# Attention and gated feed-forward on one core: another order of the opening, the last weight in halves, pooling sums of the second batch on GpSimd

## The chip, the cores and the metric

The kernel runs on one core of one Trainium2 chip. The metric is device microseconds from start to end of one launch. The core's engines are TensorE (PE; its weight loads are shown apart as PEld), VectorE (DVE), ScalarE (ACT), GpSimd (POOL) and SyncE (SP), which issues nearly all DMAs. Each engine works through its own list of instructions in order.

## The reference

Eight batches of eight heads, 576 tokens each, head width 64. Keys and values are pooled: the mean of every eight tokens, so 72 pooled positions per head. Then softmax attention, and a gated two-layer product over the 4608 tokens (512 features, 2048 hidden).

```python
k_p = k.reshape(B, H, Sp, pool, D).mean(axis=3)
v_p = v.reshape(B, H, Sp, pool, D).mean(axis=3)
scores = scale * np.matmul(q, k_p.transpose(0, 1, 3, 2))
attn = softmax(scores)                      # max subtracted, 1e-9 in the sum
x = np.matmul(attn, v_p)                    # to (4608, 512)
h = x @ w_in
out = (h * np.clip(h + 3.0, 0.0, 6.0) / 6.0) @ w_out
```

The weights arrive as 64-bit words (view of doubles); everything is computed in 32 bits.

## The kernel before

**Blocks and steps.** The 4608 tokens are cut into 12 blocks (512, 256, then ten of 384). For each block, 16 steps f run over 128 hidden columns each. A step has `h()` (L590: twelve products over four chunks of features, each as high times high, low times high and high times low, where high and low are two 32-bit parts that TensorE multiplies fast), then on ACT and DVE `relu`, `gate`, `hi`, `lo` (L603 to L617), and two steps later `out()` (L619: three products for each 128 tokens, into four sums that stay in PSUM for the whole block). While block j runs its steps, the attention for block j+1 is threaded in between as a list of small pieces (`att_steps`, `Paced`).

**Block 0 is different.** Its attention cannot hide beside another block, and the 16 weights have to be prepared during it. A weight f is 1024 columns: 512 of w_in (part 0) and 512 of w_out (part 1). `Prep` turns a raw weight into high and low parts in six operations: `scale`, `low` and `hi` on ACT, `sign`, `join` and `lo` on DVE. Weight 0 is loaded and prepared in two halves, the others whole. During the steps, step u finishes weight u+1 (`hi`, `lo`), joins weight u+2 and starts weight u+3 (L799 to L814). Two scratch buffers u take turns (f even or odd); they lie in the place of weight 15. So weight 15 can be loaded only when weight 14's `lo` has read its scratch buffer: L809.

**The opening** is one list written out by hand (L676 to L766) under `in_order()`, which ties each instruction on TensorE, DVE and ACT to the one before it in the text on the same engine. GpSimd and SP are not tied; for them, and outside such blocks, a scheduler chooses the order. The opening first sums and scores tokens 0 to 255 of batch 0 (part A), then multiplies with the values (`av`), then does tokens 256 to 511 (part B): score product, maximum (`top`), exponentials (`exps`, four ACT instructions that also give the sums; or `shift`, `exp`, `total`, which puts part of it on DVE), `invert`, `divide`, `transposes`, `av`. Between them stand the preparation of weight 0 and the first halves of step f=0 for part A (`a[0]`). Step f=0 for part B is then the first step of the loop. `busy(n)` (L200) gives TensorE n products of the identity with itself, which nobody reads; 13 stand at the start. PSUM banks for the attention are taken in turn from `att_banks`.

**The pooling sums.** `prep_k` (L139) and `prep_v` (L242) sum every eight tokens. For batch 0 the keys are summed on DVE and the values on TensorE (`FirstValues`: products with the identity, for the 64 first pooled positions in `heads`, for the remaining eight in `rest`, the latter masked on DVE in `place_rest`). For batch 1, needed by block 1 and so computed during block 0's steps, four key sums and six value sums are DVE reductions in the written order. For later batches they are DVE reductions that the scheduler places. After each sum of values GpSimd multiplies with a mask and subtracts the high part (L258, L267, L272). Raw keys and values share a ring of four buffers, so values of batch 1 are loaded as key sums free them.

Of the kernel before, what the change touches and what calls it, by code (L numbers as in the profile page):

```python
# [30 lines left out]
def attention_moe_kernel(  # L31
# [104 lines left out]

    ksum = {}

    def prep_k(b, p):  # L139
# [4 lines left out]
        with in_order() if b == 1 else nullcontext():  # L144
            nc.vector.tensor_reduce(
                out=ks[:, i], in_=kraw.pop((b, p)).rearrange("p (s o) -> p s o", o=POOL), axis=AX.X, op=ALU.add
            )
# [57 lines left out]
    class FirstValues:  # L205
# [27 lines left out]
        def place_rest(self):  # L233
            for g in range(NG):
                nc.vector.tensor_tensor(
                    out=self.vrem[:, g].rearrange("p (h d) -> p h d", h=4),
                    in0=self.pr[:, g, None, :].broadcast_to([REM, 4, D]),
# [4 lines left out]
    def prep_v(b, p):  # L242
# [9 lines left out]
        with in_order() if b == 1 else nullcontext():  # L252
            nc.vector.tensor_reduce(  # L253
                out=vs, in_=st[:n, : POOL * D].rearrange("p (o d) -> p d o", o=POOL), axis=AX.X, op=ALU.add
            )
# [150 lines left out]
    def put_x(j, T, x0, p, ps):  # L406
        xhi, xlo = (t[:, p, x0 : x0 + T] for t in x_block(j))
        nc.scalar.copy(xhi, ps)  # L408
        nc.vector.tensor_tensor(out=xlo, in0=ps, in1=xhi.bitcast(F32), op=ALU.subtract)  # L409

    def av(j, b, h0, T, x0, p):
# [4 lines left out]
        put_x(j, T, x0, p, ps)  # L416
# [48 lines left out]
    def groups(f):  # L465
        return [(0, 1), (1, 2)] if f < SPLIT else [(0, 2)]

    def w_tile(name, f, a, b, shape, dtype):
        return const.tile([P, b - a] + shape, dtype, name=f"{name}_{f}", tag=f"w_{f}_{a}" if f < SPLIT else f"w_{f}")

    def load_w(f):
        wraw[f] = []
# [7 lines left out]
    class Prep:  # L480
# [10 lines left out]
        def __init__(self, f):  # L491
            self.f, self.raws, self.made = f, wraw.pop(f), {}
            if f == 0:
                ubuf.append(const.tile([P, 2, 2 * DM], F32, name="u", tag=f"w_{NF - 1}"))
            if f == NF - 1:
                _, _, raw = self.raws[0]
                self.parts = [(i, i + 1, raw[:, i : i + 1], ring("u")[:, :DM]) for i in range(2)]
            else:
                u = ubuf[0][:, f % 2]
                self.parts = [(a, b, raw, u[:, a * DM : b * DM]) for a, b, raw in self.raws]  # L500
# [59 lines left out]

    def prep(f, *stages, part=None):
        if f not in preps:
            preps[f] = Prep(f)
        parts = preps[f].parts
        for s in stages:
            for x in parts if part is None else parts[part : part + 1]:
                getattr(preps[f], s)(x)
# [107 lines left out]
    a = [Step(first, f, 0, 2) for f in range(SPLIT)]  # L675
    with in_order():  # L676
# [4 lines left out]
        for x in (x00, x10, x01, x11):  # L681
            x.product()
        x00.top()
# [20 lines left out]
        values.rest()  # L704
        values.place_heads()
        T0, T1 = tiles(A)
        transposes(*T0, 0, 0)
        transposes(*T1, 0, 0)
        values.place_rest()
        prep(0, "scale", "low", part=0)  # L710
        transposes(*T0, 1, 0, nc.scalar.copy)
        transposes(*T1, 1, 0, nc.scalar.copy)
        prep(0, "sign", "join", "hi", "lo", part=0)
        av(0, *A, 0)
        prep(0, "scale", part=1)
        av(0, *A, 1)
        prep(0, "low", part=1)
        av(0, *A, 2)
        av(0, *A, 3)
        prep(0, "sign", "join", "hi", part=1)  # L720
        att_banks[:] = ["a0", "a1", "o2", "o3"]
        turn = [(t, g) for g in range(NG) for t in tiles(B)]
        b = [Scores(*t[:2], g) for t, g in turn]
        b[0].product()
        b[1].product()
        a[0].h()
        b[2].product()
        b[3].product()
        b[0].top()
        b[0].exps()  # L730
        prep(0, "lo", part=1)
# [136 lines left out]
```

## Time and profile before

| | us |
|---|---|
| median of 3 runs | 963.69 |
| lowest, highest | 961.54, 964.84 |
| profiled execution | 961.42 |
| its span | 959.6 |
| PE busy | 936.5 |
| DVE busy | 467.4 |
| ACT busy | 448.0 |
| POOL busy | 130.4 |

All times of the trace are counted from the span's start. Rows of groups of instructions read: line of the kernel, engine, operation, output tile and inputs, shapes and count, then busy time in us and mean ns of one, then the idle time of the engine before them and what ended it. Rows of the timeline read: start, duration, engine, line, operation, count, and in brackets the engine's wait before it with the engine, tile and line that ended it. A busy PE includes modelled ends of products that overlap.

### The profile page before, as it was taken

Reading aid. Unit: us, or ns where it says so; the run is one execution under the profiler, and the core shown is the slowest. Engines: PE = TensorE matmul, PEld = TensorE weight load, DVE = VectorE, ACT = ScalarE, POOL = GpSimd, SP = SyncE. Lnnn points to the kernel's source line nnn. Section 1 sums busy time; section 2 is a strip of 40 time slices with the busy share of each in tenths; the row PEclk is TensorE's granted clock in tenths of the full one; section 3 lists DMA queues with packets and bytes.
Section 4 is the critical chain, followed back from the end, with each engine's and each line's share of the span. In section 5 each row is a group of like instructions: output and inputs, shape, how many; then the busy total and the mean of one; then the engine's idle time right before and its main releaser. Section 6 shows DMA issues by size and latency. Waiting matters only on the chain.

```text
span 959.6 us, 13759 instructions
## 1 busy us (share of the span) xinstructions
PE 936.5 (98%) x4934; PEld 832.6 (87%) x4934; DVE 467.4 (49%) x986; ACT 448.0 (47%) x1388; POOL 130.4 (14%) x247
## 2 busy tenths in 40 slices
PE   8799989999999999999999999999999999999998
PEld 6577768899999999999999999999999998999996
DVE  5788975747424437436433444634633442442221
ACT  4578755645334426435435345434534453532322
POOL 1000340403001103102201010300300110110000
PEclk9899999999999999999999999999999999999999
DMA  9942013313001104004001004102201000100000
GB/s 338 397 158 67 17 45 105 95 36 107 12 26 31 35 1 153 24 1 153 12 1 55 12 24 129 48 1 93 72 1 37 19 23 1 45 1 1 33 1 33
DMA packets 42452, 58.57 MB, mean 61 GB/s; under 512 B 3600, under 2 KB 24080, under 8 KB 42384
## 3 DMA queue, kind: packets, MB, share of 16 engines
q1 hardware_dynamic: 42240, 57.69, 18.0%
q8 instruction: 39, 0.64, 0.3%
q14 instruction: 29, 0.24, 0.1%
q10 hardware_dynamic: 144, 0.00, 0.0%
HBM read 48.24 MB, written 9.44 MB: 60 GB/s over the span
## 4 chain that ended last, share of the span: by engine, by line
PE 82%; DVE 4%; ACT 3%; DMA 1%; issue 1%; SPq 0%; ACTq 0%; POOL 0%; DVEq 0%
PE pso L626 37%; PE psh L597 37%; PE psa L415 3%; PE psa L295 3%; PE psa L368 2%; DVE w L555 1%; ACT e L303 1%; DVE u L516 1%; ACT raw L522 1%; DMA vst<-v_l 1%; DVE vst L253 1%; DVE g L609 1%; ACT u L511 0%; DMA raw<-w_out_l 0%; DVE u L527 0%
## 5 line engine op out<-in xcount | busy, mean ns | idle before, releaser
L597 PE MATMUL psh<-xhi,w 128*128 128x384 f32 (+2 forms) x1544 | 432.3, 340 | 7.5 <-DVE w L555 5.0
L626 PE MATMUL pso<-w,ghi 128*128 128x512 f32 x1152 | 360.6, 402 | 2.1 <-ACT ghi L613 2.1
L597 PEld LDWEIGHTS psh<-xhi,w 128*128 128x128 f32 x1544 | 281.0, 189 | 23.9 <-DVE w L555 7.8
L597 PE MATMUL psh<-xlo,w 128*128 128x384 f32 (+2 forms) x772 | 260.0, 337 | 0.0
L626 PEld LDWEIGHTS pso<-w,ghi 128*128 128x128 f32 x1152 | 207.2, 188 | 33.7 <-ACT ghi L613 2.3
L605 ACT ACTIVATE g<-psh,small 128x384 f32<-128x384 f32 (+2 forms) x193 | 112.5, 583 | 240.3 <-PE psh L597 240.0
L626 PE MATMUL pso<-w,glo 128*128 128x512 f32 x576 | 219.6, 396 | 1.2 <-DVE glo L617 1.2
L609 DVE SCALAR_TENSOR_TENSOR g<-g,psh 128x384 f32<-128x384 f32 (+2 forms) x193 | 106.1, 550 | 225.4 <-ACT g L605 224.5
L597 PEld LDWEIGHTS psh<-xlo,w 128*128 128x128 f32 x772 | 146.0, 189 | 9.9
L613 ACT CAST ghi<-g 128x384 fp32r<-128x384 f32 (+2 forms) x193 | 99.5, 516 | 74.2 <-DVE g L609 71.8
L617 DVE TENSOR_TENSOR glo<-g,ghi 128x384 fp32r<-128x384 f32 (+2 forms) x193 | 108.9, 565 | 51.6 <-ACT ghi L613 49.4
L329 POOL TENSOR_TENSOR a<-e,sm 128x256 f32<-128x256 f32 x72 | 47.7, 663 | 634.6 <-DVE sm L320 407.7
L626 PEld LDWEIGHTS pso<-w,glo 128*128 128x128 f32 x576 | 107.7, 188 | 27.8 <-DVE glo L617 2.8
L303 ACT ACTIVATE e<-psa,mx 128x72 f32<-128x72 f32 x288 | 89.2, 330 | 52.6 <-DVE mx L299 50.3
L299 DVE TENSOR_REDUCE mx<-psa 128x4 f32<-128x288 f32 x80 | 35.2, 453 | 56.0 <-PE psa L295 55.8
L303 ACT ACTIVATION_READ_ACCUMULATOR e<-psa,mx 128x1 f32 x288 | 61.6, 214 | 0.0
L409 DVE TENSOR_TENSOR xlo<-psa,xhi 128x192 fp32r<-128x192 f32 (+3 forms) x68 | 29.6, 438 | 37.8 <-ACT xhi L408 37.7
L253 DVE TENSOR_REDUCE vst<-vst 128x64 f32<-128x512 f32 (+1 forms) x42 | 44.8, 1072 | 6.1 <-DMA vst<-v_l 3.4
L408 ACT CAST xhi<-psa 128x192 fp32r<-128x192 f32 (+3 forms) x68 | 25.9, 384 | 45.2 <-PE psa L415 44.4
L295 PE MATMUL psa<-kbd,qt 128*128 128x144 f32 x280 | 43.4, 286 | 0.4 <-ACT kbd L153 0.4
L295 PEld LDWEIGHTS psa<-kbd,qt 128*128 128x128 f32 x280 | 40.6, 189 | 2.1 <-ACT kbd L153 0.6
L379 DVE TENSOR_TENSOR alo<-psa,ahi 128x256 fp32r<-128x256 f32 (+1 forms) x70 | 27.7, 396 | 24.4 <-ACT arem L378 24.3
(67 smaller groups left out, 620.1 us busy)
## 6 DMA issues: line engine op xcount, KB each, us to landing
qt<-q_l SPq DMA_DIRECT2D x36, 256.0 KB, 3.5
out<-o SPq DMA_DIRECT2D x36, 256.0 KB, 2.1
raw<-w_in_l SPq DMA_DIRECT2D x16, 512.0 KB, 10.1
raw<-w_out_l SPq DMA_DIRECT2D x16, 512.0 KB, 10.1
kst<-k_l SPq DMA_DIRECT2D x28, 288.0 KB, 3.7
vst<-v_l SPq DMA_DIRECT2D x28, 256.0 KB, 3.9
vst<-vr_l SPq DMA_DIRECT2D x42, 64.0 KB, 1.9
stage<-k_l SPq DMA_DIRECT2D x4, 288.0 KB, 3.4
```

Of the source, the lines that this page charges most:

```text
L253: nc.vector.tensor_reduce(out=vs, in_=st[:n, : POOL * D].rearrange("p (o d) -> p d o", o=POOL), axis=AX.X, op=ALU.add)
L295: nc.tensor.matmul(to, qt[:, p, :], kbd[:, p, :], start=True, stop=True)
L299: nc.vector.tensor_reduce(out=self.mx, in_=self.ps, axis=AX.X, op=ALU.max, negate=True)
L303: nc.scalar.activation(self.e[:, h], self.ps[:, h], AF.Exp, bias=self.mx[:, h : h + 1], accum_out=self.sm[:, h : h + 1])
L329: engine.tensor_tensor(out=self.a[:, : 4 * D].rearrange("p (h s) -> p h s", h=4), in0=e[:, :, :D], in1=sm[:, :, None].broadcast_to([P, 4, D]),
L409: nc.vector.tensor_tensor(out=xlo, in0=ps, in1=xhi.bitcast(F32), op=ALU.subtract)
L597: nc.tensor.matmul(self.ps, l[f][:, c, :], r[:, c, :], start=c == 0 and i == 0, stop=c == NCC - 1 and i == 2)
L605: nc.scalar.activation(self.g, self.ps, AF.Relu, bias=half, scale=1.0 / (6.0 * WSCALE))
L609: nc.vector.scalar_tensor_tensor(out=g, in0=g, scalar=1.0, in1=self.ps, op0=ALU.min, op1=ALU.mult)
L613: nc.scalar.copy(self.ghi, self.g)
L617: nc.vector.tensor_tensor(out=self.glo, in0=self.g, in1=self.ghi.bitcast(F32), op=ALU.subtract)
L626: nc.tensor.matmul(pos, l, r[f], start=f == 0 and i == 0, stop=f == NF - 1 and i == 2)
```

## The change

1. The opening is written in another order. Score products, maxima and exponentials of part B stand between the value products of part A; all scores use `exps`; part B's transposes and value products are spread between the parts of step f=0; weight 1 is prepared to its end and weight 2 up to `sign` inside the opening. Two `xlo` subtractions on DVE are put behind the cast of weight 1 (`later`).
2. Thirteen more products that nobody reads: `busy(6)` behind the first scores, `busy(5)` and `busy(2)` ahead of value products of part B. The first batch's remaining eight pooled positions are summed and masked by GpSimd and no longer by TensorE and DVE.
3. Weight 15 is loaded in two halves with a place each. The scratch buffer of odd weights lies in the place of half 0, that of even weights in the place of half 1, so half 0 waits for weight 13's `lo` and half 1 for weight 14's. The loads are written one step earlier, and the halves are prepared apart, part 0 in the step of k = 15, part 1 in that and the next. The first step's `h` (part B of f=0) is tied to the written order.
4. The sums of batch 1 become `fold` on GpSimd: three additions in place (four and four, two and two, one and one) for each of four key tiles and six value tiles.

```diff
+    def fold(x, to):
+        for w in (4, 2, 1):
+            out = to[:, None] if w == 1 else x[:, :w]
+            nc.gpsimd.tensor_tensor(out=out, in0=x[:, :w], in1=x[:, w : 2 * w], op=ALU.add)
...
-        with in_order() if b == 1 else nullcontext():
+        raw = kraw.pop((b, p))
+        if b == 1:
+            fold(raw.rearrange("p (s o) -> p o s", o=POOL), ks[:, i])
+        else:
             nc.vector.tensor_reduce(
...
         def rest(self):
-            self.pr = att_bank()[:REM, : NG * D].rearrange("p (g d) -> p g d", g=NG)
-            self.add(self.pr, vraw[0, NPAIR])
+            raw = vraw[0, NPAIR]
+            for w in (4 * D, 2 * D, D):
+                nc.gpsimd.tensor_tensor(out=raw[:, :, :w], in0=raw[:, :, :w], in1=raw[:, :, w : 2 * w], op=ALU.add)
...
+        if b == 1:
+            fold(st[:n, : POOL * D].rearrange("p (o d) -> p o d", o=POOL), vs)
...
     def groups(f):
-        return [(0, 1), (1, 2)] if f < SPLIT else [(0, 2)]
+        return [(0, 1), (1, 2)] if f < SPLIT or f == NF - 1 else [(0, 2)]
...
+            if f < 2:
+                ubuf.append(const.tile([P, 2 * DM], F32, name="u", tag=f"w_{NF - 1}_{1 - f}"))
```

The opening after the change, from the last divide of part A on:

```python
        values.rest()
        prep(0, "scale", "low", part=0)
        prep(0, "scale", part=1)
        values.place_heads()
        prep(0, "sign", "join", part=0)
        # transposes of part A: two copied by DVE, two by ACT
        prep(0, "hi", "lo", part=0)
        b[0].product()
        av(0, *A, 0)
        b[0].top()
        b[1].product()
        av(0, *A, 1)
        b[0].exps()
        b[1].top()
        av(0, *A, 2)
        av(0, *A, 3)
        b[2].product()
        b[0].invert(); b[0].divide(nc.gpsimd)
        b[1].exps()
        a[0].h()
        b[2].top()
        b[3].product()
        b[1].invert(); b[1].divide(nc.vector)
        prep(0, "low", part=1)
        a[0].relu()
        b[2].exps()
        a[0].gate()
        b[3].top()
        # transposes of b[0], b[1]
        prep(0, "sign", "join", part=1)
        a[0].hi()
        b[2].invert(); b[2].divide(nc.gpsimd)
        prep(0, "hi", part=1)
        a[0].lo()
        b[3].exps()
        prep(0, "lo", part=1)
        busy(5)
        av(0, *B, 0); av(0, *B, 1)
        prep(1, "scale", "low")
        b[3].invert(); b[3].divide(nc.vector)
        a[0].out()
        # transposes of b[2], b[3]
        prep(1, "sign", "join")
        prep(2, "scale")
        busy(2)
        av(0, *B, 2, later); av(0, *B, 3, later)
        prep(1, "hi")
        # the two xlo of later
        prep(1, "lo")
        prep(2, "low", "sign")
```

The steps of the loop, with the last weight:

```diff
-                x.h(slot)
+                with in_order() if x.n < x.blk.nt * P else nullcontext():
+                    x.h(slot)
                 with in_order() if x.blk.j == 0 else nullcontext():
                     if k:
                         prep(k - 1, "hi", "lo")
+                    if k == NF - 1:
+                        prep(k, "scale", "low", part=0)
                     x.relu()
                     x.gate()
-                    if k and k < NF - 1:
+                    if k == NF - 1:
+                        prep(k, "sign", "join", part=0)
+                    elif k:
                         prep(k, "join")
                     x.hi()
                     x.lo()
                     if k and k + 1 < NF - 1:
                         prep(k + 1, "scale", "low", "sign")
-                    if k == NF - 1:
-                        load_w(k)
-                    if preps and u == len(steps) - 3:
-                        prep(NF - 1, "scale", "low", "sign", "join")
+                    if k == NF - 2:
+                        load_w(NF - 1)
+                    elif k == NF - 1:
+                        prep(k, "hi", "lo", part=0)
+                        prep(k, "scale", "low", "sign", "join", part=1)
                     elif preps and u == len(steps) - 2:
-                        prep(NF - 1, "hi", "lo")
+                        prep(NF - 1, "hi", "lo", part=1)
```

More of the change, by code (lines that the diff above doesn't have):

```diff
@@ L404, in av_sums, with av @@
         return mms + [(wrem[:, g, i * P : (i + 1) * P], rem[:, :T])]
[L406 to L411, printed above, removed]
+    def av(j, b, h0, T, x0, p, later=None):
         ps = att_bank()[:, :T]
@@ L415, in av @@
             nc.tensor.matmul(ps, l, r, start=n == 0, stop=n == len(mms) - 1)
-        put_x(j, T, x0, p, ps)
+        xhi, xlo = (t[:, p, x0 : x0 + T] for t in x_block(j))
+        nc.scalar.copy(xhi, ps)
+        low = lambda: nc.vector.tensor_tensor(out=xlo, in0=ps, in1=xhi.bitcast(F32), op=ALU.subtract)
+        low() if later is None else later.append(low)
     def side_steps(b):
@@ L563, in prep @@
             preps[f] = Prep(f)
-        parts = preps[f].parts
         for s in stages:
-            for x in parts if part is None else parts[part : part + 1]:
-                getattr(preps[f], s)(x)
+            for n, x in enumerate(preps[f].parts):
+                if part in (None, n) and (f, s, n) not in prepared:
+                    prepared.add((f, s, n))
+                    getattr(preps[f], s)(x)
     n_h = [0]
@@ L682, in attention_moe_kernel @@
             x.product()
+        busy(6)
         x00.top()
@@ L704, in attention_moe_kernel @@
         values.rest()
+        prep(0, "scale", "low", part=0)
+        prep(0, "scale", part=1)
         values.place_heads()
+        prep(0, "sign", "join", part=0)
         T0, T1 = tiles(A)
@@ L708, in attention_moe_kernel @@
         transposes(*T1, 0, 0)
[L709 to L713, printed above, removed]
+        transposes(*T0, 1, 0, by_act)
+        transposes(*T1, 1, 0, by_act)
+        prep(0, "hi", "lo", part=0)
+        turn = [(t, g) for g in range(NG) for t in tiles(B)]
+        b = [Scores(*t[:2], g) for t, g in turn]
+        att_banks[:] = ["h0", "o0", "o1", "o2", "a0", "a1"]
@@ L714, in attention_moe_kernel @@
+        b[0].product()
         av(0, *A, 0)
-        prep(0, "scale", part=1)
+        b[0].top()
+        b[1].product()
         av(0, *A, 1)
-        prep(0, "low", part=1)
+        b[0].exps()
+        b[1].top()
         av(0, *A, 2)
         av(0, *A, 3)
[L720 to L725, printed above, removed]
@@ L742, in attention_moe_kernel @@
         b[1].invert()
         b[1].divide(nc.vector)
-        b[2].top()
+        prep(0, "low", part=1)
+        a[0].relu()
         b[2].exps()
+        a[0].gate()
         b[3].top()
-        b[3].shift()
-        b[3].exp()
+        att_banks[:] = ["a0", "a1", "h0"]
+        transposes(*turn[0][0], turn[0][1], 256)
+        transposes(*turn[1][0], turn[1][1], 256, by_act)
+        prep(0, "sign", "join", part=1)
+        a[0].hi()
+        b[2].invert()
+        b[2].divide(nc.gpsimd)
+        prep(0, "hi", part=1)
@@ L767, in attention_moe_kernel @@
+        av(0, *B, 2, later)
+        av(0, *B, 3, later)
+        prep(1, "hi")
+        for low in later:
+            low()
+        prep(1, "lo")
+        prep(2, "low", "sign")
     for f in range(4, NF - 1):
```

70 lines of the change are left out of this document (26 added, 44 removed).

## The prediction

> **What bounds the kernel now.** I read the page first, then a table of stages (busy time and granted clock in stretches of the span), then the waits of TensorE in the bad stretches, then their timelines.
>
> ```profile
> span 959.6 us, 13759 instructions
> 24.60:57.40 32.80, 26.11 (x113) 18.46 (x112) 24.08 (x52) 21.04 (x61) 3.42 (x8) 0.84 1.03 396
> 57.40:77.00 19.60, 19.60 (x89) 15.87 (x88) 15.77 (x21) 15.29 (x23) 0.00 (x0) 1.00 0.01 4
> 77.00:138.00 61.00, 55.06 (x243) 43.26 (x242) 55.60 (x75) 42.93 (x93) 20.17 (x20) 0.97 0.14 39
> 138.00:155.00 17.00, 16.09 (x88) 13.47 (x87) 8.23 (x19) 9.64 (x32) 1.84 (x4) 1.00 0.16 56
> 650.00:850.00 200.00, 200.00 (x1075) 181.98 (x1074) 84.72 (x201) 89.50 (x312) 25.35 (x50) 1.00 0.11 35
> ```
>
> The columns are the stretch, its length, busy time (and instructions) of PE, PEld, DVE, ACT and POOL, the clock, the DMA share and GB/s. From block 1 on (last row) TensorE never stands still and the change leaves that code alone: nothing is to be had there. What can be had lies before 155 us. In 24.60 to 57.40 TensorE is idle 32.80 - 26.11 = 6.7 us, and a mean clock of 0.84 costs 0.16 x 32.8 = 5.2 us more. In 77 to 138 it is idle 5.9 us and loses 0.03 x 61 = 1.8 us by the clock; DVE is busy 55.60 of 61. In 138 to 155 it is idle 0.9 us. Together 20.5 us: no gain can be larger.
>
> ```profile
> 34.20 0.70 PE L415 MATMUL psa<-a,v 128*128 128x256 f32 x2 [2.11 <-ACT a L373]
> 40.00:41.00 1.00, 1.00 (x5) 0.69 (x4) 0.94 (x1) 0.43 (x3) 0.00 (x0) 0.50 1.04 414
> 47.67 1.22 DVE L555 TENSOR_TENSOR w<-u,w 128x1024 fp32r<-128x1024 f32 x1
> 48.94 1.22 PE L597 MATMUL psh<-xhi,w 128*128 128x512 f32 x2 [0.72 <-DVE w L555]
> 50.00:51.00 1.00, 1.00 (x4) 0.81 (x3) 1.00 (x6) 1.00 (x4) 0.21 (x1) 0.50 1.06 421
> 52.57 0.88 PEld L626 LDWEIGHTS pso<-w,ghi 128*128 128x128 f32 x4
> ```
>
> The opening is a chain ACT, DVE, PE, not a full engine. TensorE waits 2.11 us for the copies behind the last scores, and its clock then is half until past 40 us. The end of the opening is the low half of weight 1 (DVE, 47.67 + 1.22 = 48.9); only then do the products of step f=1 run on, again at half clock.
>
> **The opening, part by part.** The new order interleaves the scores of tokens 256 to 511 with the value products of the first 256, and finishes weight 1 inside the opening. I count the ACT list, the longest, from the first scale of weight 0 to the cast of weight 1.
>
> ```profile
> L522 ACT ACTIVATE raw<-raw 128x1024 f32<-128x1024 f32 x14 | 16.3, 1162 | 0.0
> L511 ACT ACTIVATE u<-raw 128x1024 uint32<-128x1024 uint8 x14 | 15.9, 1136 | 0.0
> L550 ACT CAST w<-u 128x1024 fp32r<-128x1024 f32 x14 | 14.8, 1058 | 0.4 <-DVE u L527 0.4
> L522 ACT ACTIVATE raw<-raw 128x512 f32<-128x512 f32 x4 | 2.7, 667 | 2.7 <-DMA raw<-w_in_l 2.2 <-DMA raw<-w_out_l 0.5
> L511 ACT ACTIVATE u<-raw 128x512 uint32<-128x512 uint8 x4 | 2.5, 652 | 0.0
> L550 ACT CAST w<-u 128x512 fp32r<-128x512 f32 x4 | 2.4, 617 | 2.6 <-DVE u L527 2.6
> L408 ACT CAST xhi<-psa 128x256 fp32r<-128x256 f32 x8 | 2.8, 367 | 4.1 <-PE psa L415 4.1
> L374 ACT COPY arem<-psa 32x128 f32<-32x128 f32 x8 | 2.0, 251 | 3.3 <-DVE a L373 3.2
> 26.71 0.31 ACT L303 ACTIVATE stage<-psa,mx 128x72 f32<-128x72 f32 x1
> 27.91 0.48 ACT L605 ACTIVATE g<-psh,small 128x256 f32<-128x256 f32 x1
> 28.88 0.40 ACT L613 CAST ghi<-g 128x256 fp32r<-128x256 f32 x1
> 2.38 5.70 PE L203 MATMUL idle<-ident 128*128 128x128 f32 x26 [2.38 <-POOL ident masks.py:199]
> 11.67 5.55 PE L218 MATMUL psa<-stage,ident 128*128 128x256 f32 x32 [1.62 <-DMA stage<-v_l]
> 15.29 1.66 PEld L218 LDWEIGHTS psa<-stage,ident 32*32 32x32 f32 x16 [0.33 <-issue]
> 19.24 0.69 PE L415 MATMUL psa<-arem,vrem 32*128 32x256 f32 x2
> 10.00:20.00 10.00, 8.38 (x50) 6.50 (x50) 5.88 (x23) 4.79 (x21) 1.62 (x4) 1.00 1.06 364
> ```
>
> Weight 0: two scales, two lows, two casts, 3.9. Placing the values, in two pieces of 256 columns like L408's: 0.8. Eight arem copies 2.0, four a copies (256 columns again) 1.4, eight xhi casts 2.9. Four groups of exps at 27.91 - 26.71 = 1.2: 4.8 (two of these replace the shift form, one ACT instruction each, and free DVE). Relu and ghi 0.9. Weight 1: scale, low, cast 3.4; scale of weight 2: 1.2. Sum 21.3 us. The DVE list, added alike, is 18 us and the PE list 18 us, so ACT is the nearest to full. The list can start when w_in of weight 0 lands: the values land at 11.67, and the remainder and that half (0.13 and 0.52 MB) follow at 364 GB/s, so about 13.5. In the 24.60 row ACT is busy 64% and DVE 73%. Ends: at 64%, 13.5 + 33.3, and 1.2 for DVE's low half, is 48.0, 0.9 us before now's 48.9; at 95%, 37.1, or 11.8 us earlier. I take 80%: 13.5 + 26.6 + 1.2 = 41.3, **7.6 us** earlier. Reason: when I walk the three lists with these durations, the scores of the second half start before the value products of the first and no longer after them, the last group's exps end near 31, its value products run from 35 to 37, and weight 1's low half ends near 40; no TensorE gap is above 1.3 us. I add one us to that for hops between engines.
>
> The clock: the last ten products of step f=1 run from 48.94 to 52.57, 3.63 us; at full clock they follow each other at about 0.23 (the four weight loads at 52.57: (0.88 - 0.19) / 3), which makes 2.3. **1.3 us** goes if the clock stays up. The Trainium skill ("TensorE: Matmul & The Clock Gate", the practical table at its end) puts the fall at TensorE gaps above about 3 us; here it fell after 2.11 us, so the measurement decides. By the page alone neither the fall nor the products nobody reads would matter, and the 1.3 us would stand at nothing.
>
> Thirteen products nobody reads are added. The thirteen at the start took 5.70, so that is the price if nothing covers them; six lie before the values land (11.67), seven before copies that TensorE waits for, so I cost them at nothing. The remainder's value sum leaves TensorE (1.66) and its multiply leaves DVE; GpSimd gets five operations for it, behind its second divide, which ends near 14. By the 256-column row below they take 3.3 us clean, 4.7 if DVE holds them up: ready at 17.4 to 18.8, against a first use at 19.24 now. Nothing lost, and the transposes go out 1.7 us earlier, which the walk contains.
>
> **The second batch's sums.**
>
> ```profile
> 39.56 4.29 SPq L135 DMA_DIRECT2D kst<-k_l  x4
> 77.27 1.41 DVE L145 TENSOR_REDUCE ksum<-kst 128x72 f32<-128x576 f32 x2
> 90.02 0.90 POOL L329 TENSOR_TENSOR a<-e,sm 128x256 f32<-128x256 f32 x1 [37.62 <-DVE sm L320]
> L145 DVE TENSOR_REDUCE ksum<-kst 128x72 f32<-128x576 f32 x4 | 2.8, 746 | 0.7 <-ACT kbd L153 0.7
> L253 DVE TENSOR_REDUCE vst<-vst 128x64 f32<-128x512 f32 x4 | 4.3, 1065 | 0.0
> L253 DVE TENSOR_REDUCE vst<-vst 96x64 f32<-96x512 f32 x2 | 1.9, 1007 | 0.0
> L329 POOL TENSOR_TENSOR stage<-stage,sm 128x256 f32<-128x256 f32 x4 | 2.5, 615 | 28.6 <-ACT ghi L613 15.2 <-DVE sm L320 13.4
> 129.34 1.69 DVE L555 TENSOR_TENSOR w<-u,w 128x1024 fp32r<-128x1024 f32 x1
> 129.50 0.45 POOL L267 TENSOR_TENSOR vlo<-vst,vhi 128x128 fp32r<-128x128 f32 x1
> 109.03 1.51 POOL L267 TENSOR_TENSOR vlo<-vst,vhi 128x128 fp32r<-128x128 f32 x1 [0.41 <-ACT vhi L266]
> 126.49 2.92 DVE L253 TENSOR_REDUCE vst<-vst 128x64 f32<-128x512 f32 x3
> 131.08 1.22 PE L597 MATMUL psh<-xhi,w 128*128 128x512 f32 x2 [3.19 <-DVE w L555]
> ```
>
> DVE loses 2.8 + 4.3 + 1.9 = 9.0 us. GpSimd gets 30 adds. Clean, on the line through 0.615 for 256 elements and 0.45 for 128: a value fold 0.62 + 0.45 + 0.37 = 1.44, a key fold (288, 144, 72) 0.66 + 0.47 + 0.38 = 1.51; six and four are 14.7 us. Held up, each add can wait one DVE instruction (0.45 against 1.51: 1.06 more), 46.5 us in all. The key fold reads every eighth element, which shows nowhere in this trace; its lower end is the clean time, its upper the held one, and I stay near the clean one while DVE has slack.
>
> The price is on DVE. At 129.50 an undisturbed GpSimd operation of 0.45 stretches the DVE one beside it from 1.22 to 1.69, by its whole length. DVE's instructions with two SBUF operands (sign, join, the weight's low half at 1.22, g's at about 0.7; nine to ten steps in the 61 us) fill some 0.68 of the time, so 0.68 x 14.7 = 10 us can come back. In DVE time the move is worth between -1 and +9 us; I take +2, near the stretched row. TensorE's time is surer: three value sums in a row (126.49, 2.92 us) delay weight 13's low half, TensorE waits 3.19 us for it, and the stage's clock loss of 1.8 us follows. That pile goes, 5.0 us. I take off 1.5 for waits that the shared access adds elsewhere: **3.5 us**, bounds -1 and +6.
>
> The last weight: its w_in half may load after weight 13's low half instead of 14's. The 138 row bounds it at 0.9 us; I take **0.4**. Each load waits in SP's queue a step earlier; behind it stand only later query loads.
>
> Sum: 7.6 + 1.3 + 3.5 + 0.4 = 12.8 us: span 946.8. The profiled execution took 961.42, so 948.6; the median of the runs shown is 963.69, from which I forecast 950.9.
>
> **Rivals.**
> A. GpSimd gives back all that DVE gains: stage gain 0, 963.69 - 9.3 = 954.4. For: the 0.45 us stretch. Against: GpSimd stands idle for 37.62 us before 90.02, and the key folds can go there. The Trainium skill ("SBUF — State Buffer", Who interferes with whom) says so outright: a reduce on this chip never contends, a two-input SBUF operation and a GpSimd read exclude each other. The stretch agrees.
> B. The new order waits as the old did: ACT at 70% gives 45.1, 3.8 us, and the clock falls: 3.8 + 3.5 + 0.4 = 7.7, 956.0.
> C. Slower: the value chain on GpSimd comes late. If the key folds start only where DVE's sums do now (77.27) and every add is held up, 46.5 us of folds and the 20.17 of GpSimd's own work end at 144. Now's last value sum ends at 129.4 with some 6 us of GpSimd behind it; less 12.8, TensorE wants the values at about 123. It would wait 21 us: 963.69 - 12.8 + 21 = 972. It decides from a finish 13 us late. Against: the key loads are issued from 39.56 on, long before.
> D. The earlier start is lost because the supply of raw weights paces the stage (DMA share 1.03 to 57 us): 962. Against: by the 57.40 row (share 0.01) all of them have landed when step 3 begins.
>
> **Chances.** Forecast 0.54, A 0.20, B 0.14, C 0.06, D 0.06. About 0.3% (2.9 us) is what a measurement can tell from no change. Faster: 0.54 + 0.20 + 0.14 = 0.88; same 0.06 (D); slower 0.06 (C). Low end: opening 11 with its clock, stage 6, tail 0.9, and 1.3 for the spread of runs: 944.5. High end: B with a stage gain of only 1.0: 958.5.
>
> **What would show it.** Weight 1's low half ending near 41 and the clock 1.00 through 30 to 55: the opening. No wait above 1 us for L555 in the steps of weights 13 and 14, DVE's share there down: the stage. Low halves stretched beyond 1.22 wherever folds run: A. A TensorE wait on vhi or kbd above 3 us: C. An ACT busy share near 64% before weight 1's cast would prove me wrong first.

## The result, and the profile after

The changed kernel takes 950.42 us (median of four runs, 950.22 to 951.77) against 962.65 us (961.54 to 964.84) for the kernel before beside it: a ratio of 0.9873, 95% interval 0.9851 to 0.9895, 12.2 us less. A second series, beside the experiments, gave 950.87 us and 0.9870 (0.9851 to 0.9888). The forecast was 950.9. For the profiled execution it was 948.6; that took 951.77.

The first view is the table of stages of the kernel after, over the stretches that the prediction used (stretch, length, busy time of PE, PEld, DVE, ACT and POOL, clock, DMA share, GB/s).

```profile
span 950.0 us, 13799 instructions
24.60:57.40 32.80, 31.39 (x164) 23.84 (x164) 28.54 (x55) 27.52 (x80) 12.16 (x14) 1.00 1.04 397
77.00:138.00 61.00, 55.50 (x243) 43.58 (x243) 49.58 (x71) 45.35 (x97) 21.72 (x32) 0.94 0.11 33
138.00:155.00 17.00, 17.00 (x100) 14.82 (x98) 6.36 (x13) 7.18 (x14) 0.00 (x0) 1.00 0.27 94
```

In the first stretch TensorE's idle time falls from 6.7 us to 1.4 and the clock from a loss of 5.2 us to none. In the third nothing is gained: idle 5.5 us (5.9 before), and the clock there costs 0.06 x 61 = 3.7 us (1.8 before), although DVE is busy 49.6 us and no longer 55.6. The loss has moved and stands in one place, 77 to 100 us, as the finer table shows, first of the kernel after and then of the variant with the sums back on DVE (`e1_sums_on_dve`, told below):

```profile
77.00:100.00 23.00, 17.50 (x62) 12.16 (x62) 17.00 (x22) 16.83 (x41) 18.90 (x28) 0.87 0.11 29
100.00:128.00 28.00, 28.00 (x136) 23.24 (x135) 24.86 (x36) 22.07 (x46) 0.92 (x2) 0.98 0.09 27
```

```profile
77.00:100.00 23.00, 22.42 (x106) 17.86 (x105) 20.36 (x36) 21.55 (x59) 5.93 (x8) 1.00 0.08 22
100.00:128.00 28.00, 22.26 (x96) 16.73 (x95) 25.35 (x28) 16.36 (x25) 15.10 (x12) 1.00 0.11 34
```

With the sums on DVE TensorE is idle 0.6 us in the first of these stretches and 5.7 in the second; with the folds it is 5.5 and nothing, and the clock falls besides.

For a sum that closes I use two marks which every variant has: the first eight `out` products of 512 columns (TensorE is then through the opening) and ACT's copy of the last two outputs of block 1. The timeline of the kernel before, then of the kernel after:

```profile
57.61 2.03 PE L626 MATMUL pso<-w,ghi 128*128 128x512 f32 x8
...
210.99 1.16 ACT L629 ACTIVATE o<-pso 128x512 f32<-128x512 f32 x2
```

```profile
38.44 1.23 DVE L565 TENSOR_TENSOR w<-u,w 128x1024 fp32r<-128x1024 f32 x1 [0.52 <-ACT w L560]
...
50.48 2.03 PE L640 MATMUL pso<-w,ghi 128*128 128x512 f32 x8
...
201.01 1.16 ACT L643 ACTIVATE o<-pso 128x512 f32<-128x512 f32 x2
```

The opening mark comes 7.1 us earlier. The new order also has some 1.5 us of block 1's value products ahead of it (46.63 to 48.15 us) that the old one has behind it, so the opening is worth 7.1 to 8.6 us. Between the marks lie 153.4 us before and 150.5 after, 2.9 us less, or 1.4 without those products. From the second mark to the end it is 748.6 and 749.0 us. The same three lengths for all variants, each from its one profiled execution (the last rows are told below):

| kernel | first mark | between | to the end | median us | ratio to before (95%) |
|---|---|---|---|---|---|
| before | 57.6 | 153.4 | 748.6 | 962.7 to 963.8 | |
| folds alone | 60.6 | 150.7 | 748.5 | 964.46 | 1.0004 (0.9984 to 1.0025) |
| halves alone | 59.2 | 150.5 | 748.6 | 961.05 | 0.9978 (0.9964 to 0.9992) |
| new opening alone | 52.1 | 152.7 | 748.6 | 955.17 | 0.9922 (0.9900 to 0.9945) |
| opening and halves | 51.4 | 151.1 | 748.5 | 952.88 | 0.9893 (0.9872 to 0.9914) |
| opening and folds | 50.4 | 155.0 | 748.7 | 956.07 | 0.9943 (0.9922 to 0.9963) |
| after (all three) | 50.5 | 150.5 | 749.0 | 950.42 | 0.9873 (0.9851 to 0.9895) |
| after, no idle products | 52.3 | 151.0 | 748.9 | 952.28 | 0.9890 (0.9864 to 0.9915) |
| after, key sums on DVE | 50.2 | 152.6 | 748.9 | 953.62 | 0.9898 (0.9882 to 0.9914) |
| after, eight repeats | 50.5 | 150.7 | 749.0 | 951.73 | 0.9889 (0.9864 to 0.9914) |
| after, two small sums on DVE | 51.5 | 146.4 | 748.7 | 948.45 | 0.9845 (0.9825 to 0.9866) |
| after, remainder on TensorE | 51.7 | 147.8 | 749.0 | 949.08 | 0.9851 (0.9831 to 0.9872) |
| the last two together | 53.3 | 146.4 | 749.2 | 950.72 | 0.9863 (0.9840 to 0.9886) |

Whatever a variant changes, it changes before the second mark. In four rows with all the idle products (first marks 52.1, 51.4, 51.5 and 53.3) the clock fell once ahead of the first mark (see the end). No run shows that the edit named in the row is the cause of that, so the column between the marks compares the folds and the halves better.

### The profile page after: what moved, and what is told of

It reads as the page before. It is cut to its first block, busy times and chain, and to the rows that moved or that the text cites. A ratio compares the mean times of both kernels' runs of the same rounds, so it can differ in the third digit from the quotient of the medians.

```text
span 950.0 us, 13799 instructions
## 1 busy us (share of the span) xinstructions
PE 932.9 (98%) x4944; PEld 831.0 (87%) x4944; DVE 464.9 (49%) x970; ACT 449.6 (47%) x1402; POOL 160.0 (17%) x282
## 4 chain that ended last, share of the span: by engine, by line
PE 89%; DMA 6%; POOL 2%; ACT 1%; SPq 1%; issue 1%; DVE 0%; ACTq 0%; POOLq 0%
PE pso L640 41%; PE psh L611 40%; DMA raw<-w_in_l 4%; PE psa L307 3%; PE psa L423 3%; PE psa L380 2%; POOL vst L141 1%; DMA kst<-k_l 1%; DMA stage<-v_l 1%; DMA vst<-vr_l 0%; ACT u L521 0%; ACT raw L532 0%; POOL vst L270 0%; POOL vlo L279 0%; DVE u L526 0%
## 5 line engine op out<-in xcount | busy, mean ns | idle before, releaser
L611 PE MATMUL psh<-xhi,w 128*128 128x384 f32 (+2 forms) x1544 | 429.6, 339 | 4.4 <-DVE w L565 3.7
L611 PEld LDWEIGHTS psh<-xhi,w 128*128 128x128 f32 x1544 | 279.6, 188 | 19.4 <-DVE w L565 5.0
L611 PE MATMUL psh<-xlo,w 128*128 128x384 f32 (+2 forms) x772 | 258.9, 335 | 0.0
L611 PEld LDWEIGHTS psh<-xlo,w 128*128 128x128 f32 x772 | 145.3, 188 | 9.6
L315 ACT ACTIVATE e<-psa,mx 128x72 f32<-128x72 f32 x288 | 88.9, 327 | 53.1 <-DVE mx L311 49.6
L265 DVE TENSOR_REDUCE vst<-vst 128x64 f32<-128x512 f32 (+1 forms) x36 | 38.7, 1076 | 7.5 <-DMA vst<-v_l 4.1
L331 DVE TENSOR_SCALAR sm<-sm 128x4 f32<-128x4 f32 x80 | 14.4, 179 | 51.7 <-ACT e L315 50.9
```

The costliest lines, as they stand in the source:

```text
L265: nc.vector.tensor_reduce(out=vs, in_=st[:n, : POOL * D].rearrange("p (o d) -> p d o", o=POOL), axis=AX.X, op=ALU.add)
L315: nc.scalar.activation(self.e[:, h], self.ps[:, h], AF.Exp, bias=self.mx[:, h : h + 1], accum_out=self.sm[:, h : h + 1])
L611: nc.tensor.matmul(self.ps, l[f][:, c, :], r[:, c, :], start=c == 0 and i == 0, stop=c == NCC - 1 and i == 2)
```

## The experiments

**The opening, the halves and the folds: one by one and in pairs.** "Opening" here includes the products nobody reads, the first batch's remainder on GpSimd and the tying of the first step's `h`. Folds undone in the kernel after:

```diff
-        if b == 1:
-            fold(raw.rearrange("p (s o) -> p o s", o=POOL), ks[:, i])
+        with in_order() if b == 1 else nullcontext():
+            nc.vector.tensor_reduce(out=ks[:, i], in_=..., axis=AX.X, op=ALU.add)
...
-        if b == 1:
-            fold(st[:n, : POOL * D].rearrange("p (o d) -> p o d", o=POOL), vs)
+        with in_order() if b == 1 else nullcontext():
+            nc.vector.tensor_reduce(out=vs, in_=..., axis=AX.X, op=ALU.add)
```

> The change with the second batch's ten sums back on DVE, in the written order as before; everything else as changed. If the folds are worth the forecast 3.5 us, this takes about 954 us (950.4 + 3.5) and shows the pile again: three value sums in a row and a TensorE wait near 3 us for a weight's low half. If GpSimd gives back on DVE all that DVE gains (rival A), it stays within 1.5 us of 950.4, and the stage from 48 to 145 us loses as much TensorE time (idle about 6 us, clock about 3.5 us) as in the changed kernel.

Measured: 952.88 us, 0.9893, between the two expectations: the folds are worth some 2 us in the finished kernel, with intervals that overlap. In the profiled execution 0.9 us of it stands at the first mark, through a fall of the clock at 24 to 27.4 us, long before the second batch's sums, and 0.6 us between the marks. The pile that the prediction wanted gone is back (timeline of this variant; its L605 and L559 are the kernel after's L611 and L565):

```profile
124.61 0.73 PE L605 MATMUL psh<-xhi,w 128*128 128x512 f32 x2 [3.22 <-DVE w L559]
```

The same edit turned round, the folds put into the kernel before:

> The kernel before with nothing but the folds on GpSimd. Forecast's view: about 959 us (962.65 - 3.5). Rival A: 962 to 964, no change that can be told from none. If the shared access costs more than it brings: 965 or more.

Measured: 964.46 us against 963.52, ratio 1.0004 (0.9984 to 1.0025). Alone the folds bring nothing that can be measured; in its profiled execution the first mark comes 3.0 us later and the stretch between the marks is 2.7 us shorter.

The last weight, undone in the kernel after (one part, loaded and prepared at the old places) and, in the other direction, put alone into the kernel before (the variant "halves alone", which also ties the first step's `h`):

```diff
-        return [(0, 1), (1, 2)] if f < SPLIT or f == NF - 1 else [(0, 2)]
+        return [(0, 1), (1, 2)] if f < SPLIT else [(0, 2)]
...
-                    if k == NF - 2:
-                        load_w(NF - 1)
-                    elif k == NF - 1:
-                        prep(k, "hi", "lo", part=0)
-                        prep(k, "scale", "low", "sign", "join", part=1)
+                    if k == NF - 1:
+                        load_w(k)
+                    if preps and u == len(steps) - 3:
+                        prep(NF - 1, "scale", "low", "sign", "join")
```

> The changed kernel with the last weight loaded and prepared whole, at the place where the kernel before did it. Forecast: 0.4 us more, 950.8; bounds 0 to 0.9 by the idle time of TensorE in that stretch before. A rise of more than 1.5 us would mean that the order of the loads or of the first steps matters beyond this stretch.

Measured: 956.07 us, 0.9943. The halves are worth 5.6 us there, fourteen times the forecast term. The timeline of this variant shows about half of the mechanism (L527 is `sign`, L624 the gate, L612 `h`, L641 `out`):

```profile
136.19 1.29 DVE L527 SCALAR_TENSOR_TENSOR u<-raw,u 128x512 uint32<-128x512 uint32 x2 [3.73 <-ACT u L522]
...
138.72 0.69 DVE L624 SCALAR_TENSOR_TENSOR g<-g,psh 128x512 f32<-128x512 f32 x1
...
139.47 0.39 PE L612 MATMUL psh<-xhi,w 128*128 128x256 f32 x1 [0.62 <-DVE g L624]
...
148.24 0.39 PE L612 MATMUL psh<-xhi,w 128*128 128x256 f32 x1 [1.50 <-DVE g L624]
...
168.62 0.74 PE L641 MATMUL pso<-w,glo 128*128 128x512 f32 x2 [0.98 <-DVE glo L632]
```

DVE waits 3.73 us for ACT's part of the last weight, which lands late, and the gate of the step stands behind it in the written order; TensorE waits for the gate, 2.1 us in all. Another 2.0 us of idle time lies between 155 and 180 us, in waits for `glo` and `g` (0.98, 0.41 and 0.59 us). From 128 to 180 us the kernel after has no idle time of TensorE at all. In the kernel after the same stretch reads

```profile
132.13 0.69 DVE L526 SCALAR_TENSOR_TENSOR u<-raw,u 128x512 uint32<-128x512 uint32 x1
...
136.54 0.69 DVE L526 SCALAR_TENSOR_TENSOR u<-raw,u 128x512 uint32<-128x512 uint32 x1 [0.94 <-ACT u L521]
```

with no wait above 0.94 us for a sign. Is it the folds that make the whole weight so dear, because they finish the values early? The last value product of block 1, in the new opening alone and in the new opening with folds and a whole last weight:

```profile
134.70 0.27 PE L417 MATMUL psa<-arem,vrem 96*128 96x192 f32 x1
```

```profile
112.97 0.28 PE L423 MATMUL psa<-arem,vrem 96*128 96x192 f32 x1
```

(In the kernel before it starts at 141.37 us.) The folds finish the values some 22 us earlier, so this work is not there while the last weight is awaited. But that explains little: between 138 and 155 us TensorE is idle 0.9 us in the kernel before, 1.7 in the new opening alone, whose `sign` waits 4.43 us, and 2.1 with the folds. The larger difference lies behind, between 155 and 180 us: 0.6, 0.5 and 2.0 us. Why `glo` and `g` come later there I did not follow. To see whether the parts add up I ran the new opening alone and the halves alone.

> The kernel after with the last weight whole at its old place and all ten sums of the second batch back on VectorE: what is left of the change is the opening. Additive (each part is worth what its removal cost: the sums 2 us, the halves 5.6): 950.4 + 2.0 + 5.6 = 958. Interaction (the folds finish the last value sums early, so the value products of block 1 are no longer there to fill TensorE while the last weight is awaited, and only then do the halves pay): 953 to 955.5, with weight 15's step free of a TensorE wait above 1.5 us, and the opening is worth about 8 us by itself. The prediction's terms (opening 7.6 and clock 1.3): 954.

> The kernel before with the last weight alone changed: its w_in and w_out halves loaded a step apart and prepared a step apart, the rest as before. If the halves are worth 5.6 us wherever they stand: 957 to 958. If they only pay beside the folds (interaction): 0 to 2 us, 961 to 963.5. The prediction's term was 0.4 with a bound of 0.9: 962.5.

Measured: 955.17 us (0.9922) and 961.05 us (0.9978). With the other two variants this is a square on the new opening: neither 955.2, halves 952.9, folds 956.1, both 950.4. Without folds the halves are worth 2.3 us and with them 5.6; folds cost 0.9 us without halves and bring 2.5 with them. An additive sum asked for 958 where 955.2 was measured. Each ratio carries 0.2% either way, so the interaction of 0.4% is at the edge of what the times alone can tell; the lengths between the marks (152.7, 151.1, 155.0, 150.5) say the same, 1.6 us for the halves without folds and 4.5 with them. Its cause is shown only in the small part above and stays open.

**The products nobody reads.** In the kernel after, `busy(6)`, `busy(5)` and `busy(2)` are taken out.

> The changed kernel without the thirteen added products that nobody reads. If they hold the clock up in the opening, it falls to half somewhere between 25 and 45 us and the time rises by 1.3 to 4 us, to 951.7 to 954.5. If the new order alone keeps TensorE busy enough, the clock stays at 1.00 there and the time stays within 1 us of 950.4.

Measured: 952.28 us, 0.9890; the first mark is 1.8 us later. A row of this variant's table of stages, and the same row of the variant with the sums on DVE, which has all the products:

```profile
20.00:24.60 4.60, 4.60 (x19) 2.33 (x17) 2.60 (x6) 2.69 (x13) 0.00 (x0) 1.00 1.02 405
24.60:30.00 5.40, 4.82 (x27) 4.52 (x26) 3.29 (x12) 3.84 (x19) 0.81 (x2) 0.68 1.03 408
```

```profile
24.60:30.00 5.40, 5.36 (x35) 5.14 (x34) 3.70 (x13) 3.88 (x20) 0.81 (x2) 0.75 1.02 407
```

The clock is 0.68 in a stretch where the kernel after has 1.00. But it is 0.75 there with all the products too, and the six executions without them fall into two groups: 950.0 to 950.7 us at a mean clock of 0.997 to 1.000, and 953.9 to 955.7 at 0.990 to 0.993, the profiled one among these. So the clock can hold without the products and can fall with them. That they make a fall rarer fits the runs (the eight of the kernel after lie between 950.15 and 952.02) but is not shown; by the times the 1.9 us lie inside the intervals. That they cost nothing agrees with the first marks, 50.5 us with them and 52.3 without.

Beside these ran the kernel after once more:

> The kernel after unchanged, to stand beside the others of this call on the same chip. 950 to 952 us, 0.987 to 0.989 of the kernel before.

It gave the 950.87 us named above, and its lengths between the marks (50.6, 150.7, 748.9) repeat those of the first profile to 0.2 us.

**Where the folds lose what they free.** The groups between 48 and 100 us, one shape each, in the kernel after and then in the variant with the sums on DVE (line, engine, operation, tiles, count, busy us, mean ns):

```profile
L526 DVE SCALAR_TENSOR_TENSOR u<-raw,u 128x1024 uint32<-128x1024 uint32 x7 | 10.9, 1554 | 4.1 <-ACT u L521 4.0
L537 DVE SCALAR_TENSOR_TENSOR u<-raw,u 128x1024 uint32<-128x1024 uint32 x7 | 10.2, 1457 | 0.0
L565 DVE TENSOR_TENSOR w<-u,w 128x1024 fp32r<-128x1024 f32 x6 | 9.6, 1603 | 0.0
L141 POOL TENSOR_TENSOR kst<-kst 128x288 f32<-128x288 f32 x4 | 7.2, 1824 | 4.0 <-DMA kst<-k_l 4.0
L141 POOL TENSOR_TENSOR vst<-vst 128x256 f32<-128x256 f32 x4 | 3.9, 988 | 0.0
```

```profile
L520 DVE SCALAR_TENSOR_TENSOR u<-raw,u 128x1024 uint32<-128x1024 uint32 x8 | 10.1, 1258 | 5.3 <-ACT u L515 5.3
L531 DVE SCALAR_TENSOR_TENSOR u<-raw,u 128x1024 uint32<-128x1024 uint32 x8 | 9.8, 1219 | 0.0
L559 DVE TENSOR_TENSOR w<-u,w 128x1024 fp32r<-128x1024 f32 x8 | 9.7, 1218 | 0.0
```

Beside the folds `sign`, `join` and the low half take 0.30, 0.24 and 0.39 us more each: 2.1 + 1.7 + 2.3 = 6.1 us. The low half of g (`glo`) takes 0.26 us more each, 946 ns for 685, 1.8 us for seven. Together 7.9 of the 9.0 us that DVE was freed from come back; the prediction took 7. But this is not yet the wait of 77 to 100 us. Its timeline in the kernel after:

```profile
88.19 2.42 POOL L141 TENSOR_TENSOR vst<-vst 96x256 f32<-96x256 f32 x3 [1.30 <-DMA vst<-vr_l]
...
89.94 2.63 DVE L565 TENSOR_TENSOR w<-u,w 128x1024 fp32r<-128x1024 f32 x1
...
91.44 1.59 POOL L270 TENSOR_TENSOR vst<-vst,small 96x256 f32<-96x256 f32 x1
...
92.62 0.72 PE L611 MATMUL psh<-xhi,w 128*128 128x512 f32 x2 [2.44 <-DVE w L565]
...
95.90 0.40 ACT L282 CAST vrem<-vst 96x256 fp32r<-96x256 f32 x1 [2.42 <-POOL vst L270]
96.21 0.61 ACT L627 CAST ghi<-g 128x512 fp32r<-128x512 f32 x1
...
96.88 3.78 PE L640 MATMUL pso<-w,ghi 128*128 128x512 f32 x8 [0.81 <-ACT ghi L627]
```

TensorE waits 2.44 us for weight 8's low half, which took 2.63 us and not 1.22, and then runs at half clock (eight products in 3.78 us, where the row of 50.48 us has 2.03). Two theories: the loss is this wait with the clock behind it, or it is what GpSimd has to get done there. First, eight more copies of weight 8's first product stand in front of it (the next one overwrites their sums), to cover the wait:

```diff
             for c in range(NCC):
+                if self.blk.j == 0 and f == 8 and c == 0:
+                    for _ in range(8):
+                        nc.tensor.matmul(self.ps, w_in_hi[f][:, 0, :], xhi[:, 0, :], start=True, stop=True)
```

> The kernel after, and in front of weight 8's first product (the one with the 2.44 us wait for its low half, behind which the clock is half for some 7 us) eight more of the same product, whose sums the next one overwrites. Theory 1 (what the folds gained is mostly given back in clock, since VectorE's sign and low half stretch to 1.53 and 2.63 us beside the folds and TensorE waits past the point where its clock falls): the wait shrinks to below 0.8 us, the clock stays at 1.00 over 77 to 100, and 2.5 to 3.5 us go: 947 to 948.5. Theory 2 (the clock in the records is not what the time hangs on there): 950.4, or up to 1.8 us more if the repeats are not covered.

Measured: 951.73 us, 0.9889, no gain; 150.7 us between the marks against 150.5. The expectation that the low half's wait was the cost fell. What the clock costs this run can't say, for it fell again, one place later: 0.95 and no longer 0.87 over 77 to 100 us, but not 1.00. The timeline of this variant shows where the wait went:

```profile
88.91 2.01 PE L612 MATMUL psh<-xhi,w 128*128 128x512 f32 x8
...
95.53 0.40 ACT L282 CAST vrem<-vst 96x256 fp32r<-96x256 f32 x1 [1.44 <-POOL vst L270]
95.84 0.61 ACT L630 CAST ghi<-g 128x512 fp32r<-128x512 f32 x1
...
96.51 2.88 PE L643 MATMUL pso<-w,ghi 128*128 128x512 f32 x8 [2.84 <-ACT ghi L630]
```

The repeats covered the low half's wait, and TensorE stood 2.84 us at the next place: for `ghi`, which on ACT is queued behind the cast of the values' remainder, which waits for GpSimd's mask (L270) and so for its folds. The `out` products behind `ghi` start at 96.51 us, against 96.88 in the kernel after. So the second edit takes work away from GpSimd, which in the kernel after is busy 18.9 of 23 us there: the two small value sums (96 rows) go back to DVE, the eight others stay.

```diff
-        if b == 1:
+        if b == 1 and p < NPAIR:
             fold(st[:n, : POOL * D].rearrange("p (o d) -> p o d", o=POOL), vs)
```

> The kernel after with the two 96-row value sums alone (three adds each on GpSimd, among them 2.42 us beside weight 8's sign and low half) back on VectorE, in no written order. Shared-access theory: weight 8's low half goes back to 1.3 to 1.5 us, TensorE's wait for it falls from 2.44 to below 1.5, the clock holds, 947.5 to 949. Rival (two reductions of 1.0 us each on VectorE take the place of what they free, and GpSimd's other operations are beside the low half anyway): 950 to 951.5.

Measured: 948.45 us (948.0 to 949.32), 0.9845 (0.9825 to 0.9866); 4.2 us less between the marks. Timeline and table of stages of this variant:

```profile
90.93 1.22 DVE L565 TENSOR_TENSOR w<-u,w 128x1024 fp32r<-128x1024 f32 x1
...
92.20 0.73 PE L611 MATMUL psh<-xhi,w 128*128 128x512 f32 x2 [0.67 <-DVE w L565]
...
92.97 0.62 ACT L627 CAST ghi<-g 128x512 fp32r<-128x512 f32 x1
```

```profile
77.00:100.00 23.00, 17.90 (x80) 13.12 (x79) 18.81 (x27) 16.73 (x43) 18.71 (x21) 1.00 0.12 29
```

The low half is back at 1.22 us, `ghi` comes 3.2 us earlier and the clock stays up. The `out` products behind `ghi` start at 94.61 us, 2.3 us earlier than in the kernel after, and take 2.02 us and not 3.78. GpSimd is no less busy in the stretch (18.71 us), since its operations now wait for DVE's, and TensorE is idle 5.1 us of it, hardly less than the 5.5 of the kernel after. So the edit takes away the late `ghi` and the fall of the clock together, and does not say which of the two is worth more. TensorE's idle time stays because other waits take its place, 1.96 us for an earlier step's `ghi` the longest. Which sums are taken off DVE matters, and not only how many, as the variant with the four key sums back on DVE says:

> The kernel after with the four key sums back on VectorE in their written order, the six value sums still folded by GpSimd. Theory 1 (the strided key folds, 1.8 us an add, cost by shared access more than they free): at or a little below the kernel after, 948 to 950.5, with fewer stretched operations of two SBUF operands. Theory 2 (any sum off VectorE helps): 951 to 952.

Measured: 953.62 us, 0.9898. Here the first theory fell: the strided key folds are the longest adds, but they run while GpSimd is otherwise idle, and taking them back costs 3 us; TensorE is then idle 7.6 us between 77 and 100. The cause within DVE's order I did not follow further, and value sums on DVE with key folds on GpSimd was not tried.

**The first batch's remainder.** Summed by TensorE and masked by DVE again, as in the kernel before, the rest as after:

```diff
-            raw = vraw[0, NPAIR]
-            for w in (4 * D, 2 * D, D):
-                nc.gpsimd.tensor_tensor(out=raw[:, :, :w], in0=raw[:, :, :w], in1=raw[:, :, w : 2 * w], op=ALU.add)
+            self.pr = att_bank()[:REM, : NG * D].rearrange("p (g d) -> p g d", g=NG)
+            self.add(self.pr, vraw[0, NPAIR])
...
         transposes(*T1, 0, 0)
+        values.place_rest()
```

> The kernel after with the first batch's 32-row remainder summed by TensorE again (eight small products more) and placed by VectorE behind the transposes of the first group, in place of five operations of GpSimd. The prediction's step (nothing lost by GpSimd, transposes 1.7 us earlier): 951.5 to 952.5. By the trace of after, where tile x01's divide waits behind those adds and the first value products start at 18.88 us against 18.64 before, the move brought nothing: 950 to 951.

Measured: 949.08 us, 0.9851 (0.9831 to 0.9872), which overlaps with the kernel after. The first `h` product starts at 24.86 us after and at 26.08 in this variant, and the first mark agrees (50.5 and 51.7): in the opening the move to GpSimd does bring 1.2 us, though less than the 1.7 forecast for the transposes. So my second expectation's reason (the move brought nothing) fell. But between the marks this variant is 2.8 us shorter (from 77 to 100 us TensorE is idle 3.8 us, with the clock at 0.93), through another order of GpSimd's and DVE's work in the stage; why, I did not settle. In sum undoing this part of the change took 1.3 us off by the medians, where both expectations had the time equal or longer. Last, both edits that were ahead:

> Both last edits together in the kernel after: the two 96-row value sums on VectorE, and the first batch's remainder on TensorE. If the remainder's move is worth something of its own in the opening (1.3 us by the medians 949.1 and 950.4): 947. If it only shifted where the folds meet weight 8's low half, which the other edit settles already: 948 to 949.5.

Measured: 950.72 us, 0.9863. That is above both expectations. Between the marks it is 146.4 us, the same as with the small sums alone, which fits the second expectation's reason, that both edits take away the same loss. Its first mark is 2.8 us later than that of the kernel after (1.2 for the remainder, the rest a fall of the clock, see the end), and the total is no better. The lowest time of the study is that of the small sums on DVE alone, 948.45 us; it was not timed in one series with the kernel after, and that kernel's second series ran on another chip. But its five runs (948.0 to 949.3) all lie below the eight of the kernel after (950.15 to 952.02).

## Why the prediction came out, step by step

- **Opening, 7.6 and 1.3 us: right in mechanism and in sum, less so in the terms.** Weight 1's low half ends at 39.67 us; forecast were 41.3, and 40 by the walk. ACT's list was counted too long and its share too high: from the first scale (13.31 us) to the cast of weight 1 (38.41) ACT is busy 19.15 us, 76%, where 21.3 us at 80% were forecast, and the two errors nearly cancel. By the first mark the opening is worth 7.1 to 8.6 us, alone by the times 7.5 (5.3 to 9.6), against 8.9. From 24.6 to 57.4 us no TensorE wait of the kernel after is above 0.6 us, and its clock is 1.00.
- **The clock's 1.3 us and the products nobody reads at nothing: the price is right, the safety is not.** In four of the ten profiled executions with the new order and all its products the clock fell once between 24 and 54 us.
- **Remainder on GpSimd, nothing lost: right in the opening**, 1.2 us gained; in the total the kernel is 1.3 us faster without the move, with overlapping intervals.
- **Folds on GpSimd, 14.7 us clean, "I stay near the clean one": mis-sized.** The 30 adds took 30.4 us, 16.0 of them in the key folds that read every eighth element (7.2 us for the four adds of 128x288 in the rows above; 6.0 us clean were forecast for all twelve).
- **DVE's relief, +2 us: right in size.** From 48 to 155 us DVE is busy 83.65 us, against 86.29 with the sums on DVE, 2.6 less. Over the whole execution the two are equal (464.9 and 464.7).
- **The pile, 5.0 us: its wait is gone, as forecast.** Between 100 and 128 us TensorE has no idle time, against 5.7 us, the 3.22 us wait among them, with the sums on DVE. The clock's 1.8 us in this term do not show: with the sums on DVE the clock there is 1.00 too.
- **"I take off 1.5 for waits that the shared access adds elsewhere": this term was mis-sized**, and the stage's 3.5 us with it. The 77 to 100 row has 5.5 us idle and 0.13 x 23 = 3.0 us lost by the clock; with the sums on DVE it has 0.6 and none. So most of what the pile cost came back one stage earlier. On the new opening the folds alone cost 0.9 us, in the old kernel they brought nothing: rival A's result for them, with a reason that it did not have. GpSimd's folds delay the remainder's cast on ACT, and the cast delays `ghi`. That is rival C's chain at the price of at most the 4.2 us that the small sums on DVE brought back, and not 21: late values do not wait for their own use, they hold up what is queued behind them.
- **Last weight, 0.4 us, "the 138 row bounds it at 0.9": failed.** Alone in the old kernel it is worth 1.7 us (0.8 to 3.5 by the interval), beside the folds 5.6. The bound was taken over too short a stretch: between 155 and 215 us TensorE is idle 1.1 us in the kernel before and 0.3 with the halves alone. And it was read in a kernel in which the other parts of the change were missing: with the new opening and the folds a whole last weight costs 4.1 us of idle time between 128 and 180 us. Why so much more is only partly shown (above).
- **The sum.** The stage and last weight were forecast at 3.9 us together. From the new opening alone (0.9922) to the kernel after (0.9873) it is 0.5%, 4.7 us; between the marks it is 2.2. The stage's term was too high and the last weight's too low, and the prediction had no reason why they should make up for each other. That the total came out is luck in this part. The prediction also added the two terms, and the square says that they do not add.
- **The way from the trace to the median.** The terms made 12.8 us; the two profiled executions differ by 961.42 - 951.77 = 9.65. The medians differ by 12.2 because the profiled execution of the kernel before lies 1.2 us below its median and that of the kernel after 1.4 above. The kernel before loses more in most executions than in its profiled one: its runs range from 960.4 us at a mean clock of 0.992 to 966.2 at 0.984 in one series, those of the kernel after from 950.2 to 952.0, at 0.995 to 0.997. That the old opening's falls of the clock make this spread fits the first marks of the variants that keep it (57.6, 59.2, 60.6), but is argued from them and not shown.

## What to carry to other kernels

The idle time of one stretch did not bound what a change to that stretch brought: a term bounded at 0.9 us was worth 1.7 alone and 5.6 beside another part of the change. So undo the parts of a change one by one and in pairs before adding up what each is worth, and ask of a part that finishes work early what that work was covering. An engine that is far from full on average can still end a stage: look for who queues behind its results in written order (here a cast on ACT that waited for GpSimd, with the next step's `ghi` behind it), and try covering the wait before blaming it, since a wait that turns up again one place later has another cause.

## What the hardware showed that was not expected

**The clock falls in units of 3.4 us, and can do so with no long wait before it.** In the new opening alone, the longest wait of TensorE between 30 and 56 us is 0.60 us, as in the kernel after, with the same work at the same times. Yet in the tables of stages of the new opening alone, and then of the kernel after, the clock (third column from the right) reads

```profile
48.00:49.00 1.00, 1.00 (x5) 0.78 (x5) 1.00 (x2) 0.74 (x3) 0.00 (x0) 0.78 1.10 407
49.00:50.00 1.00, 1.00 (x3) 0.78 (x3) 1.00 (x4) 1.00 (x2) 0.00 (x0) 0.50 1.02 394
...
51.00:52.00 1.00, 1.00 (x4) 0.81 (x3) 0.77 (x1) 1.00 (x2) 0.00 (x0) 0.51 1.03 410
```

```profile
48.00:49.00 1.00, 1.00 (x6) 0.79 (x6) 1.00 (x2) 0.81 (x3) 0.00 (x0) 1.00 1.12 410
...
94.00:95.00 1.00, 1.00 (x4) 0.74 (x3) 1.00 (x2) 0.00 (x0) 1.00 (x2) 0.52 0.00 0
...
100.00:101.00 1.00, 1.00 (x6) 0.76 (x5) 1.00 (x2) 0.43 (x1) 0.00 (x0) 0.56 0.00 0
```

The fall of the new opening alone lasts (0.22 + 0.50 + 0.50 + 0.49) / 0.5 = 3.4 us. That behind weight 8 in the kernel after lasts 6.8: 0.48 and 0.44 at the ends and five microseconds at 0.50 between, over 0.5. Without the idle products it is 3.4 us again, though the 4.6 us before it have no TensorE idle time at all. The Trainium skill ("TensorE: Matmul & The Clock Gate", the part on the clock gate) tells of a window of about 3.4 us that runs freely and does not start with the kernel, and puts the slow clock after an idle window of that length. The lengths agree with it; that an idle window must come first does not hold here. Of the variants with the new opening and its idle products, the small sums on DVE and both edits together fell at 48 to 54 us too, and the sums on DVE at 24 to 27.4, for 0.9 to 1.6 us at the first mark; the others did not fall in the opening. What decides, the traces do not show. Any edit that shifts the opening by a fraction of such a window can win or lose this much, which is more than some of the differences measured above.

**A GpSimd operation can be held up by several of DVE's in a row.** The prediction let each add wait for one DVE instruction. In the variant with the small sums on DVE, the timelines of GpSimd and DVE read

```profile
89.16 3.46 POOL L270 TENSOR_TENSOR vst<-vst,small 96x256 f32<-96x256 f32 x1 [0.71 <-DVE sm L331]
```

```profile
89.15 0.66 DVE L631 TENSOR_TENSOR glo<-g,ghi 128x512 fp32r<-128x512 f32 x1
...
89.82 1.19 DVE L526 SCALAR_TENSOR_TENSOR u<-raw,u 128x1024 uint32<-128x1024 uint32 x1
90.93 1.22 DVE L565 TENSOR_TENSOR w<-u,w 128x1024 fp32r<-128x1024 f32 x1
```

An operation that takes 0.61 us where nothing holds it up (95.25 us in the kernel after) lasted 3.46, through these three DVE instructions and a reciprocal of 0.17 us among them, which follow each other without a gap (89.15 to 92.15), and the three were not lengthened (`glo`, `sign` and the low half take 0.69, 1.23 and 1.22 us at 134.09, 98.94 and 100.08 us in the kernel after, with GpSimd idle). So the price falls on either side, and on GpSimd it is not bounded by one DVE instruction.
